# A retention layer and a two-layer MLP on one core: new written-out orders for all engines, and no-operations spread between single matmuls

## The chip, the cores and the metric

The kernel runs on one core of a Trainium2 chip. The core has a matrix engine (TensorE, "PE" in the profile; its weight loads are shown apart as "PEld"), VectorE (DVE), ScalarE (ACT), GpSimd (POOL) and a queue engine that here only issues DMAs (SyncE, "SP"). The metric is the device time of one execution in microseconds, the median of several.

## The reference

Inputs are float32: q, k, v of shape (8, 8, 576, 64), that is 8 batches, 8 heads, 576 positions of 64 numbers; `w_in` of 512 x 2048 and `w_out` of 2048 x 512. What is computed:

```python
scores = (q @ k^T) / 8                               # per batch and head, 576 x 576
D[i, j] = gamma_h ** (i - j) if i >= j else 0        # gamma_h = 1 - 2 ** (-5 - h)
x = heads side by side of (scores * D) @ v           # 4608 tokens x 512
out = square(relu(x @ w_in)) @ w_out                 # 4608 x 512
```

No softmax stands between the two attention products, so the sum over positions can be carried as a state from one chunk of 128 positions to the next. The two products of the MLP are by far the larger part of the arithmetic.

## The kernel before, in words

**Tiling.** The 4608 tokens are cut into 36 units of 128 rows: 32 full chunks (a batch, 128 positions) and 4 units that take the last 64 positions of two batches. Two units make a group; there are 18 groups, 0 to 17. Matmuls run in fp16 with sums in float32. The weights are cast to fp16 on their way in by eight DMAs that POOL issues (L417, `w_in` and `w_out` in four blocks each) and stay on the chip.

**What a group goes through.** POOL (for groups 0 to 3 partly VectorE) scales and casts k, q and v (L455, L470, L476; in groups 0 to 3 tiles `kx`, `qx`, `vx`, L506). SP issues DMA transposes of q and k (tile `kqT`, L487). PE does the retention: scores into `psc`, masked by VectorE into `rT` (L784), states into `psS`, outputs into `psO`. All of that is matmuls of 64 x 64 quarters of the array, recorded by one helper, `quad` (L441), in tasks that hold 33 to 128 of them in groups 0 to 3. From group 4 on the work of two groups (outputs of one, scores and states of the next) is joined to one task, `f0`, of over 190 instructions; there are 13 such tasks, which the text calls long runs. `psO` is copied out as `xT` (ScalarE L845, VectorE L669).

**First product** (`x @ w_in`, transposed). In ten groups it is plain: 16 blocks of four matmuls, 256 columns wide (L1163), each pair of blocks followed by a relu on ScalarE (L1172) and a square on ScalarE or VectorE (L1179, L1181). In the eight groups of `FSET` (4, 6, 8, 10, 12, 14, 15, 16) it follows Strassen's scheme with seven products: tasks of eight matmuls, 128 columns wide (L1014), whose results ScalarE (L1023) copies and VectorE (L1042) adds.

**Second product** (`g @ w_out`). Group 0 is plain (512 columns wide, L1201, sixteen matmuls for a unit); all others follow Strassen's scheme with matmuls of 256 columns, two to a task (L1256), whose left sides VectorE sums (L1229) and whose results ScalarE (L1271, L1332) copies and VectorE (L1281) adds into `o`; SP stores it (L957, L962).

**Order.** The kernel's functions put 1848 tasks on a list: for each an engine, a function that emits its instructions, the tasks that it needs, the buffers that it acquires and frees, and `size`, the count of its PE instructions (a weight load and a matmul each count). `Schedule.emit` calls the functions in the order of a constant, `ORDER`, which names the tasks by number. The engines take their own instructions in that order and wait on semaphores for those of others; the buffers (eight PSUM banks in pool `ff`, rings of `xT`, `gT`, `kqT` and so on) are given out in the same order.

**No-operations.** `place_runs` goes through the PE tasks in order. Ahead of each long run it takes the next number of `PADS` and spreads so many no-operations (`filler`, an instruction of PE's queue, L335) over the small tasks since the run before: those of `size` up to 8, from the fiftieth PE task on. `emit` writes a task's share as one burst behind the task. In the kernel before, 373 no-operations lie ahead of the first, fifth, twelfth and thirteenth run.

Of the kernel before, what the change touches and what calls it, by code (L numbers as in the profile page):

```python
# [71 lines left out]
""".split()  # L72


class Schedule:
# [45 lines left out]
    def place_runs(self, tasks):  # L121

        def spread(n, among):
            total = sum(x["dur"] for x in among)
# [1278 lines left out]
```

## Time and profile before

| | |
|---|---|
| time, median of 3 runs | 292.0 us (290.43 to 293.24) |
| profiled execution, its own time | 292.98 us |
| its span in the profile | 291.3 us |
| mean granted TensorE clock | 0.995 |
| PE | 276.6 us busy (95%), 4730 matmuls |
| VectorE | 200.8 us (69%), 405 instructions |
| ScalarE | 199.7 us (69%), 374 instructions |
| POOL | 101.1 us (35%), 133 instructions |

The profile is of one execution, whose own time lies 1.7 us above its span and 1.0 us above the median of the runs. Busy time of an engine leaves out its queue's instructions: no-operations, semaphores, branches and the issue of DMAs. Matmuls are pipelined and their ends are modelled, so neighbouring matmuls overlap in the records (a 256-wide one is drawn as 273 ns long, while the next can begin after 109 ns), and short idle times of PE are seen between starts and not in the busy share. In the tables of stretches the columns are: the stretch, its length, busy time and count of PE, PEld, DVE, ACT and POOL, the granted clock, the share of the DMA engines, and GB/s.

### The profile page before, as it was taken

What the parts mean: (1) busy time and instruction counts of PE and PEld (TensorE: products, weight loads), DVE (VectorE), ACT (ScalarE), POOL (GpSimd) and SP (SyncE); (2) the same over time, 40 slices, a digit from 0 to 9 for tenths busy, and PEclk for the clock granted to TensorE, in tenths of its full rate; (3) what the DMA queues carried; (4) which work ended last, traced back from release to release, by engine and by line L of the source; (5) the groups of instructions that cost most, each with busy time, mean ns of one, the idle gap of its engine ahead of it and who ended that gap; (6) DMA issues with size and microseconds to landing.
All of it is one profiled execution on the core that took longest, in us unless ns stands there. A gap on an engine that the chain in (4) does not pass through costs nothing.

```text
span 291.3 us, 11387 instructions
## 1 busy us (share of the span) xinstructions
PE 276.6 (95%) x4730; PEld 236.9 (81%) x4730; DVE 200.8 (69%) x405; ACT 199.7 (69%) x374; POOL 101.1 (35%) x133
## 2 busy tenths in 40 slices
PE   7997999999999999999999999999979999999993
PEld 3575767788899889989798988799959888999882
DVE  4782479998876668567847885857666886664652
ACT  6535987487749766977677578758748667887630
POOL 7560037815526533536253433442434400000000
PEclk9999999999999999999999999999999999999998
DMA  7999998989998999999699798899897901011104
GB/s 208 287 207 205 276 300 177 176 194 204 163 195 214 148 201 198 229 172 190 177 182 200 185 197 177 192 191 205 196 213 181 245 16 38 3 73 37 38 36 144
DMA packets 119153, 50.01 MB, mean 172 GB/s; under 512 B 94784, under 2 KB 113728, under 8 KB 119104
## 3 DMA queue, kind: packets, MB, share of 16 engines
q1 hardware_dynamic: 114560, 44.84, 73.0%
q0 software_dynamic: 4224, 4.19, 8.7%
q8 instruction: 38, 0.62, 0.9%
q10 hardware_dynamic: 320, 0.26, 0.4%
q14 instruction: 11, 0.09, 0.1%
HBM read 36.70 MB, written 9.44 MB: 158 GB/s over the span
## 4 chain that ended last, share of the span: by engine, by line
PE 64%; DMA 11%; DVE 11%; SPq 6%; issue 3%; ACT 2%; POOL 1%; DVEq 0%; POOLq 0%
PE po L1256 27%; PE ph L1163 18%; PE ph L1014 13%; DMA w_out<-in_moe_w_out_dram 4%; DMA kqT<-kq 2%; PE psO L441 2%; PE po L1201 2%; DMA stage<-in_v_dram 2%; DVE stage L1229 2%; DVE rT L784 2%; DMA loads<-in_v_dram 1%; SPq L399 1%; DMA out_dram<-o 1%; SPq L377 1%; DVE gT L1229 1%
## 5 line engine op out<-in xcount | busy, mean ns | idle before, releaser
L1163 PE MATMUL ph<-xT,w_in 128*128 128x256 f16 x640 | 84.4, 273 | 2.0 <-issue 1.8
L1163 PEld LDWEIGHTS <-w_in 128*128 128x128 f16 x640 | 61.1, 98 | 11.4 <-issue 2.5
L1172 ACT ACTIVATE gT<-ph 128x512 f16<-128x512 f32 x80 | 46.8, 596 | 25.3 <-PE ph L1163 25.3
L1256 PEld LDWEIGHTS <-gT 128*128 128x128 f16 x544 | 50.7, 98 | 7.6 <-issue 1.5
L1256 PE MATMUL po<-w_out,gT 128*128 128x256 f16 x272 | 45.1, 273 | 0.3 <-DVE rT L784 0.3
L1256 PE MATMUL po<-wT,gT 128*128 128x256 f16 x272 | 42.1, 273 | 0.3 <-DVE o L1281 0.3
L1256 PE MATMUL po<-wT,stage 128*128 128x256 f16 x272 | 41.8, 273 | 0.1
L1256 PEld LDWEIGHTS <-stage 128*128 128x128 f16 x408 | 37.7, 98 | 5.1 <-DVE stage L1229 0.4
L455 POOL CAST kq<-loads 128x512 f16<-128x512 f32 x28 | 19.2, 686 | 62.9 <-DMA loads<-in_k_dram 62.7
L1179 ACT ACTIVATE gT<-gT 128x512 f16<-128x512 f16 x66 | 39.6, 629 | 0.3
L1042 DVE CUSTOM_DVE_ANT_0 gT<-ph,stage 128x512 f16<-128x512 f32 x32 | 22.0, 687 | 19.4 <-PE ph L1014 14.3
L1014 PEld LDWEIGHTS <-pair_c 128*128 128x128 f16 x512 | 33.0, 98 | 2.5 <-issue 1.1
L1056 ACT ACTIVATE gT<-gT 128x1024 f16<-128x1024 f16 x32 | 33.2, 1056 | 1.3 <-DVE gT L1042 1.0
L470 POOL TENSOR_TENSOR kq<-loads,qexp 128x512 f16<-128x512 f32 x24 | 26.5, 1104 | 19.5 <-DMA loads<-in_q_dram 18.1
L476 POOL TENSOR_TENSOR v<-loads,vdec_full 128x512 f16<-128x512 f32 x24 | 28.0, 1174 | 13.9 <-DMA loads<-in_v_dram 12.7
L1229 DVE TENSOR_TENSOR stage<-gT,stage 128x512 f16<-128x512 f16 (+1 forms) x51 | 31.6, 626 | 0.6
L1023 ACT COPY stage<-ph 128x512 f32<-128x512 f32 x32 | 18.7, 587 | 11.7 <-PE ph L1014 9.9
L1014 PEld LDWEIGHTS <-w_in 128*128 128x128 f16 x384 | 24.8, 98 | 2.2 <-issue 1.0
L1281 DVE TENSOR_TENSOR o<-po,u 128x256 f32<-128x256 f32 x33 | 13.8, 421 | 17.9 <-ACT u L1271 10.9
L1271 ACT COPY u<-po 128x256 f32<-128x256 f32 x34 | 12.7, 373 | 15.6 <-PE po L1256 15.6
L1256 PE MATMUL po<-w_out,stage 128*128 128x256 f16 x136 | 22.6, 273 | 0.0
L845 ACT CAST xT<-psO 128x512 f16<-128x512 f32 x28 | 15.7, 589 | 7.8 <-PE psO L441 7.5
(111 smaller groups left out, 416.2 us busy)
## 6 DMA issues: line engine op xcount, KB each, us to landing
out_dram<-o SPq DMA_DIRECT2D x32, 256.0 KB, 3.6
loads<-in_k_dram SPq DMA_DIRECT2D x24, 256.0 KB, 4.4
loads<-in_q_dram SPq DMA_DIRECT2D x96, 64.0 KB, 3.2
loads<-in_v_dram SPq DMA_DIRECT2D x24, 256.0 KB, 4.2
w_in<-in_moe_w_in_dram POOLq DMA_DIRECT2D x4, 512.0 KB, 8.5
w_out<-in_moe_w_out_dram POOLq DMA_DIRECT2D x4, 512.0 KB, 13.7
pair_c<-in_k_dram SPq DMA_DIRECT2D x2, 512.0 KB
pair_c<-in_q_dram SPq DMA_DIRECT2D x4, 256.0 KB, 6.0
```

The source lines that it names most:

```text
L455: op(out=out_.rearrange("p (n b a d) -> p n b a d", n=2, b=2, a=2), in_=in_.rearrange("p (a n b) d -> p n b a d", n=2, a=2))
L470: nc.gpsimd.tensor_tensor(out=out_.rearrange("p (t a d) -> p a t d", t=4, a=2), in0=tile_of["q32", u].rearrange("p (a t) d -> p a t d", a= ...
L476: nc.gpsimd.tensor_tensor(out=t, in0=tile_of["v32", u], in1=vdec[kind].rearrange("p (h o) -> p h o", o=1).to_broadcast([P, H, D]), op=ALU. ...
L1014: nc.tensor.matmul(out_[:, e], lhsT=left[:, m, fi * P:(fi + 1) * P], rhs=right()[:, m], start=fresh and e == 0 and m == 0, stop=m == HK - ...
L1023: nc.scalar.copy(out=part_at[name], in_=bank(j, "a").rearrange("p e t -> p (e t)"))
L1042: nc.vector._custom_dve(TENSOR_ADD_SAT, out=g_at(s, h, j), in0=bank(j, x), in1=part_at[name].rearrange("p (e t) -> p e t", t=P), s0=3.4028 ...
L1056: nc.scalar.activation(out=t, in_=t, func=ACTF.Square)
L1163: nc.tensor.matmul(tile_of["ph", g, fb][:, j, :], lhsT=w_in16[:, m, fi * P:(fi + 1) * P], rhs=tile_of["x", g][:, m, :], start=(m == 0), st ...
L1172: nc.scalar.activation(out=tile_of["g", g][:, nf * fb:nf * (fb + 1), :], in_=tile_of["ph", g, fb], func=ACTF.Relu)
L1179: nc.scalar.activation(out=t, in_=t, func=ACTF.Square)
L1229: (nc.gpsimd if eng == "POOL" else nc.vector).tensor_tensor(out=S_(k)(sl), in0=in0(sl), in1=in1(sl), op=op)
L1256: nc.tensor.matmul(tile_of["pb", g, bank], lhsT=left(i), rhs=right[:, i, :], start=(start and i == 0), stop=(i == HF - 1), skip_group_chec ...
```

## The change

Three things change; the tasks, their functions, their dependencies and the sizes of all buffers stay.

1. `ORDER` is another order of the same 1848 tasks. On PE 707 of 853 tasks stand at another place in their engine's order, by at most 33 places; on VectorE 269 of 358, on ScalarE 258 of 367, on POOL 51 of 100 (at most 5 places) and on SP 103 of 170 (at most 16).
2. `PADS` has other numbers, in all 888 no-operations instead of 373: ahead of the first, second, fifth, tenth, eleventh, twelfth and thirteenth long run 112, 219, 109, 179, 3, 191 and 75. The list goes on with zeros.
3. The no-operations are spread otherwise. A task's share goes by its `size`, no longer by its planned duration; from the two hundredth PE task on, tasks of `size` up to 16 take a share, which brings in the Strassen first products (L1014), where before only those up to 8 did; and the share is no burst behind the task any more: each matmul of the task calls `tick`, which emits a no-operation whenever the running share has reached one.

In the changed kernel lines move down: the helper `quad` is L445, the no-operation L339, Strassen's first products L1018, plain first products L1169, the plain second product L1208, Strassen's second products L1264.

```diff
@@ -14,61 +14,61 @@
 
 
 ORDER = """
-0 34 1 2 3 35 4 5 6 36 7 8 9 70 10 71 11 37 12 76 72 13 73 78 14 38 77 79 75 40 15 16 80 81 17 18 39 74 19 314 82 20 42 21 315 83 22 41 23 24 316 25
-26 84 43 27 88 317 319 90 318 28 29 85 320 30 323 89 87 86 91 321 324 92 322 44 332 93 325 31 45 32 33 326 327 46 483 328 484 47 487 329 485 488 330
...
+0 34 1 2 3 35 4 5 6 36 7 8 9 70 10 71 11 37 12 76 72 13 73 77 14 38 78 79 75 40 15 16 80 81 17 18 39 74 19 20 314 82 42 21 83 319 315 41 22 23 316 24
+84 88 320 25 85 44 317 26 27 90 28 29 318 30 89 43 31 91 87 323 46 92 321 324 93 86 32 33 325 45 327 48 326 332 328 483 484 322 487 329 485 50 47 488
...
 """.split()
 
 
@@ -110,21 +110,25 @@
                 w["left"] -= 1
         self.place_runs([t for t in order if t["eng"] == "PE"])
         for t in order:
+            self.owed, self.step = 0.0, 2.0 * t["pad"] / max(t["size"], 1)
             t["fn"]()
-            for i in range(t["pad"]):
-                self.filler()
-
-
-    PADS = (121, 0, 0, 0, 68, 0, 0, 0, 0, 0, 0, 125, 59)
+
+    def tick(self):
+        self.owed += self.step
+        while self.owed > 0.999:
+            self.owed -= 1.0
+            self.filler()
+
+    PADS = (112, 219, 0, 0, 109, 0, 0, 0, 0, 179, 3, 191, 75, 0, 0, 0, 0, 0, 0, 0, 0, 0, 0, 0, 0, 0, 0, 0, 0, 0)
     FIRST_PAD = 50
 
     def place_runs(self, tasks):
 
         def spread(n, among):
-            total = sum(x["dur"] for x in among)
+            total = sum(x["size"] for x in among)
             until, done = 0.0, 0
             for x in among:
-                until += x["dur"]
+                until += x["size"]
                 upto = int(n * until / total + 1e-6)
                 x["pad"] += upto - done
                 done = upto
@@ -135,7 +139,7 @@
             if t["size"] > 190:
                 spread(next(pads), between or [t])
                 between = []
-            elif t["size"] <= 8 and i >= self.FIRST_PAD:
+            elif t["size"] <= (16 if i >= 200 else 8) and i >= self.FIRST_PAD:
                 between.append(t)
 
 
@@ -1013,6 +1017,7 @@
                     for m in range(HK):
                         nc.tensor.matmul(out_[:, e], lhsT=left[:, m, fi * P:(fi + 1) * P], rhs=right()[:, m],
                                          start=fresh and e == 0 and m == 0, stop=m == HK - 1, skip_group_check=True)
+                        sched.tick()
             w = [wS_done[k][j]] if k in wS_done else []
...
             users.append(p)
@@ -1070,6 +1075,7 @@
                             for m in range(NP):
                                 nc.tensor.matmul(tile_of["hp", g, fi][:, x, :], lhsT=w_in16[:, m, (fi + x) * P:(fi + x + 1) * P],
                                                  rhs=tile_of["x", g][:, m, :], start=(m == 0), stop=(m == NP - 1))
+                                sched.tick()
                         key = base + F1LEN * (JSTEP * (j if not FIRSTP else 0) + (n + x / 2) / 4 * (1 - JSTEP))
                         ts.append(add("PE", key, 0.4366, f, deps=xs + wcast_of(fi) + ts, acq=() if x else ("ff",), size=8))
                     n += 1
@@ -1162,6 +1168,7 @@
                     for m in range(NP):
                         nc.tensor.matmul(tile_of["ph", g, fb][:, j, :], lhsT=w_in16[:, m, fi * P:(fi + 1) * P],
                                          rhs=tile_of["x", g][:, m, :], start=(m == 0), stop=(m == NP - 1))
+                        sched.tick()
                 f1.append(add("PE", place((nf * fb + j) * n), 0.01 + 0.2133 * n, f,
                               deps=[T["x", u] for u in us] + wcast_of(nf * fb + j) + f1[-1:],
                               acq=("ff",) if j == 0 else (), size=8))
@@ -1200,6 +1207,7 @@
                         tile_of["po", u] = ps_ff.tile([P, DM], FP32, name="po", tag="ff")
                     nc.tensor.matmul(tile_of["po", u], lhsT=tile_of["g", g][:, fi, s * P:(s + 1) * P],
                                      rhs=w_out16[:, fi, :], start=(fi == 0), stop=(fi == NF - 1))
+                    sched.tick()
                 f2.append(add("PE", 95.9 + fi / 1000 if late else base2 + NF * s + fi, 0.216, f, deps=[sq[fi // nf]] + wcast[4 + fi // 4] + f2[-1:],
                               acq=("ff",) if fi == 0 else (), size=2))
 
@@ -1255,6 +1263,7 @@
                     for i in (2 * q, 2 * q + 1):
                         nc.tensor.matmul(tile_of["pb", g, bank], lhsT=left(i), rhs=right[:, i, :],
                                          start=(start and i == 0), stop=(i == HF - 1), skip_group_check=not start)
+                        sched.tick()
                 chain[bank] = [add("PE", at_(key + q), 0.2184, f,
                                    deps=chain.get(bank, []) + deps(q // 2) + (reads if q == 0 else []) + wT_done.get(k, []),
                                    acq=("ff",) + more if start and q == 0 else (), size=4, inside=k > 1)]
```

106 rows, old and new, of the table ORDER are left out of this document.

## The prediction

> **What bounds the kernel.** I read the engines' shares and the chain that ended last, then five stretches, then what stands in the chain beside TensorE.
>
> ```profile
> PE 276.6 (95%) x4730; PEld 236.9 (81%) x4730; DVE 200.8 (69%) x405; ACT 199.7 (69%) x374; POOL 101.1 (35%) x133
> PE 64%; DMA 11%; DVE 11%; SPq 6%; issue 3%; ACT 2%; POOL 1%; DVEq 0%; POOLq 0%
> q8 instruction: 38, 0.62, 0.9%
> ```
> ```profile
> 27.00:80.00 53.00, 52.41 (x801) 42.38 (x802) 42.46 (x70) 39.31 (x77) 22.47 (x23) 1.00 1.00 212
> 80.00:130.00 50.00, 49.16 (x984) 44.68 (x982) 33.77 (x62) 36.29 (x69) 20.38 (x24) 1.00 1.07 196
> 130.00:180.00 50.00, 49.23 (x884) 44.46 (x882) 36.10 (x66) 35.34 (x67) 21.74 (x22) 1.00 0.97 184
> 180.00:230.00 50.00, 47.86 (x958) 42.21 (x956) 35.20 (x62) 35.40 (x65) 20.08 (x24) 1.00 0.93 197
> 230.00:286.00 56.00, 55.32 (x785) 49.75 (x778) 36.34 (x74) 38.10 (x69) 2.49 (x2) 1.00 0.16 52
> ```
> The second column of a stretch is PE's busy time: from 27 to 286 us PE stands for 5.0 us of 259, at a granted clock of 1.00. The change keeps all 4730 matmuls. So the time moves by what happens to PE's gaps, and a gap anywhere counts in full. The largest:
>
> ```profile
> 212.52 0.46 PE psO L441 x48
> 212.98 1.85 PE po L1256 x16
> 214.83 0.11 PE ph L1163
> 214.94 1.82 issue
> 216.77 0.97 PE ph L1163 x7
> ```
> "issue" names no partner. The third line of the first fence does: 38 fetches, 16 KB each, for about 9,855 PE instructions are one per 256. If 64 instructions run ahead of the first of the program, both places where PE stood with no semaphore attached (17.6 and 216.8 us ended them) lie on a multiple of 256. Each border seems to ask for the block after the next: the border was passed at 211.9, the fetch ran from 214.2 to 215.3, PE went on at 216.8, 4.9 us after the border. The run of small attention matmuls (L441, some 9 ns for a weight load and its matmul) had begun at place 195 of its block; so 196 of the next 256 instructions were over in 0.9 us, the rest in 1.9 us, and the next block was not there.
>
> **What the change does to such stalls.** The no-operations before a run shift it in its block. In the new program every run of over 190 instructions starts at places 101 to 141, and at least 107 instructions of its last block are left when it ends; in the kernel before, runs ending at places 72 to 162 brought no such gap. Gain 1.8 us. Ends: 0 (another run stalls instead) and 2.0 (measured between starts).
>
> [...]
>
> **No-operations** rise from 373 to 888. Their price:
>
> ```profile
> L335 PEldq NOP  x11: 13/13/13, 220.6 to 221.3; - x11
> ```
> ```profile
> 220.34 0.61 PE L1014 MATMUL ph<-xT,pair_c 128*128 128x128 f16 x8
> 220.79 0.38 PE L1256 MATMUL po<-wT,stage 128*128 128x256 f16 x2
> 221.01 0.61 PE L1014 MATMUL ph<-xs,pair_c 128*128 128x128 f16 x8
> 221.45 1.04 PE L1163 MATMUL ph<-xT,w_in 128*128 128x256 f16 x8
> 222.33 1.04 PE L1256 MATMUL po<-wT,stage 128*128 128x256 f16 x8
> ```
> Eleven no-operations took 0.73 us from first to last: 72 ns each, although each is drawn as 13 ns; other instructions between them cost 3 to 4 ns. From start to start a 256-wide matmul takes 0.88/8 = 109 ns, a 128-wide first product (L1014) 0.45/8 = 56 ns. As long as the sequencer is ahead, no-operations cost nothing. It is at most 43 instructions ahead, and at each wait it stands until the semaphore comes, which eats the lead. The old spread put none into first products; the new one gives them the same number per matmul as the wide ones.
>
> Stretch by stretch, counted in the new order: before the second long run stand 219 no-operations among 96 first-product and 66 wide matmuls. PE needs 96 x 0.0555 + 66 x 0.109 = 12.5 us; the sequencer 219 x 0.0715 + 324 x 0.0035 = 16.8 us. It is the slower one for the whole stretch: **+4.2 us** (3.5 with cheaper other instructions, 5.5 where waits add to it). Before the 10th and 12th runs the two are even (179: 13.9 against 13.6; 191: 14.8 against 14.4), but a first product with 1.2 no-operations takes 0.09 instead of 0.0555: 56 x 0.036 = 2.0 us each if nothing of it is caught up, 0.4 to 0.8 if the wide ones give it back. 109 and 75 no-operations elsewhere cost 0 to 0.9 each. Together +1.5, ends 0 and 5. The old spread's own cost (starts late by 0.05 to 0.11 us at 217, 225 and 234) goes: -0.3.
>
> **Start.** The chain runs through POOL:
>
> ```profile
> 13.51 1.03 POOL vx L506
> 14.54 1.49 POOL w_in L417 x2
> 16.03 10.95 DMA w_out<-in_moe_w_out_dram
> ```
> ```profile
> PE po L1201 <- DMA w_out<-in_moe_w_out_dram: 1.9, 1, 1.9
> ```
> Two w_in issues now stand ahead of that vx, which waits 1.9 us for its load, so the w_out issues come up to 1.5 us sooner, unless the full DMA engines (share 1.2) eat that. And PE has 21 tasks of first matmuls, not 13, before the first w_out matmul: 8 x 0.437 = 3.5 us more cover than the 1.9 us wait. What is late next: the retention work of groups 2 and 3 behind VectorE, 10.0 of 10 us busy from 50 to 60. Its last vx of group 2 ran at 41.5 to 42.2, and PE would now want it at 41.2. So I take -1.0, ends -1.9 and 0.
>
> **Waits in the middle.** Without the fetch gap PE stands 3.2 us after 27; the page draws a matmul to 273 ns where the next could start after 109, so some 20 gaps hide up to 0.16 us each: about 6 us between starts, 5.6 of it after 60 us. I measured in both orders, for each group of matmuls, the PE work between the matmul that its input comes from and itself, less the ScalarE and VectorE instructions between by their rows (relu 0.60, copies 0.37 and 0.59, sums 0.4 to 0.7). Under 0.25 us are left in 61 of 816 places before, in 21 after. I halve the 5.6: -2.8, ends -4.2 and +1. SP's transposes and stores move by up to 16 places among the same DMAs; POOL waits 62.7 us for loads and so decides little; PE waited for a transpose only at 104.6 and 126.5 (1.0 us, within the 5.6).
>
> **Sum**, against the profiled execution's 292.98 (span 291.3 and 1.7 around it): -1.8 + 4.2 + 1.5 - 0.3 - 1.0 - 2.8 = -0.2. Its own 292.98 is 1.0 above the median of the three runs; from that median, 292.0, I forecast **291.8 us**. Within 1%, 289.1 to 294.9, is about what a measurement can't tell from no change.
>
> **Rivals.** (a) *The order wins.* At 213 to 214.8 the old kernel carried 1.4 no-operations per wide matmul with none late; if the even stretches cost nothing, the dense one 3.5, waits fall to their end and the start gives all: -1.8 + 3.5 - 0.3 - 1.9 - 4.2 = -4.7, 287.3 us. For it: the far fewer tight places. Against: 219 x 72 ns can't be hidden in 12.5 us. (b) *The sequencer starves PE, slower than before.* If waits take its lead at each first product, all of them are paid: 96 x 0.05 = 4.8, twice 2.0, 0.9 and 0.7, in all 10.4 instead of 5.7: +4.5, 296.5 us. It decides once the lead at a first product is under some 10 instructions; the lead after waits in the old kernel was 2 to 10. (c) *The orders are alike*: waits stay at 5.6, +2.6, 294.6. (d) The gap's cause is not the fetch, or a run stalls elsewhere: 293.6.
>
> [...]
>
> **Chances.** Forecast with (c) and (d) near it: same 0.41. Faster by over 1%, (a) and its neighbours: 0.31. Slower, mainly (b): 0.28. Range 287.0 to 297.0, from (a) to (b).
>
> **What would show it.** No "issue" entry over 1 us after 30 us in the chain; in the stretch after the run that in the old kernel began at 75.2 us, first products every 105 ns and no-operations 72 to 80 ns apart; that stretch 16 to 17 us from run to run; PE's first w_out matmul without a DMA wait; half the wait time elsewhere. I am wrong if no-operations cost less than 60 ns there, if VectorE makes new waits before 60 us, or if another run ends in a fetch gap.

## The result, and the profile after

The changed kernel takes 304.6 us (median of 4 runs, 302.9 to 306.2), the kernel before 292.6 us in the same comparison (4 runs, 290.4 to 293.5): ratio 1.042, 95% interval 1.032 to 1.052. It is 12 us slower, where 291.8 us in a range of 287 to 297 was forecast. Medians are of all executions; the ratios and intervals on record leave out those over 1.5% above the fastest of their kernel.

The page of the changed kernel, busy shares, instruction fetches, and the chain that ended last:

```profile
PE 291.1 (96%) x4730; PEld 246.1 (81%) x4730; DVE 204.2 (67%) x405; ACT 199.8 (66%) x374; POOL 104.3 (34%) x133
...
q8 instruction: 40, 0.66, 0.9%
...
PE 78%; DVE 10%; DMA 7%; ACT 2%; issue 1%; POOL 1%; SPq 1%; DVEq 0%
```

The same 4730 matmuls keep PE "busy" 14.5 us longer, and "issue" (time in which PE waited for nothing that the profile shows) falls from 3% to 1%: the gap of 1.8 us is gone, and something slower has come. The five stretches between long runs that have no-operations in the changed kernel show where. The table of stretches, first of the kernel before, then of the changed one (stretch, length, busy time and count of PE, and so on):

```profile
76.20:89.60 13.40, 13.20 (x185) 12.06 (x175) 11.06 (x22) 8.22 (x16) 5.63 (x7) 1.00 1.00 192
116.80:126.20 9.40, 9.40 (x123) 8.40 (x109) 5.30 (x10) 8.67 (x16) 4.39 (x5) 1.00 1.19 215
182.00:197.50 15.50, 15.18 (x181) 13.19 (x169) 10.79 (x20) 10.83 (x22) 6.63 (x7) 1.00 0.90 194
212.80:228.60 15.80, 13.97 (x173) 11.92 (x160) 11.05 (x20) 9.81 (x21) 6.48 (x9) 1.00 0.90 190
229.90:238.50 8.60, 8.47 (x105) 6.99 (x105) 7.33 (x12) 5.99 (x12) 2.49 (x2) 1.00 0.45 127
```
```profile
78.50:98.70 20.20, 20.07 (x176) 15.14 (x174) 11.06 (x22) 8.49 (x16) 11.08 (x12) 1.00 0.97 193
125.60:136.50 10.90, 10.90 (x131) 9.65 (x116) 7.36 (x12) 8.76 (x15) 5.27 (x5) 1.00 1.08 188
193.40:210.20 16.80, 16.70 (x174) 14.23 (x165) 10.54 (x20) 11.28 (x23) 7.71 (x9) 1.00 0.87 183
225.40:244.00 18.60, 18.32 (x183) 14.93 (x178) 12.03 (x22) 12.13 (x25) 5.63 (x7) 1.00 0.69 144
245.10:252.60 7.50, 7.50 (x113) 6.94 (x110) 5.73 (x10) 4.17 (x10) 0.00 (x0) 1.00 0.11 39
```

Read the length, not the busy time: the first stretch has 176 records of matmuls instead of 185 and takes 20.2 us instead of 13.4, and PE is drawn as busy for 20.07 of them, because each matmul is drawn as over 0.2 us long and so covers the pause behind it. VectorE, ScalarE and POOL have less than 0.6 of the stretch. No engine is the bound; PE's sequencer is. The no-operations of that stretch, and the matmuls of a part of it in order of time:

```profile
L339 PEldq NOP  x218: 13/13/13, 78.5 to 98.6; - x109
```
```profile
87.84 0.81 PE L1018 MATMUL ph<-xT,pair_c 128*128 128x128 f16 x6
88.59 0.39 PE L1264 MATMUL po<-wT,stage 128*128 128x256 f16 x2
88.82 1.02 PE L1018 MATMUL ph<-xT,pair_c 128*128 128x128 f16 x8
89.79 0.38 PE L1264 MATMUL po<-wT,stage 128*128 128x256 f16 x2
90.04 1.04 PE L1018 MATMUL ph<-xs,pair_c 128*128 128x128 f16 x8
```

218 no-operations from 78.5 to 98.6 us are one every 92.6 ns, and eight first products take 0.97 us (88.82 to 89.79) where eight took 0.45 before. With the records put in the order of the program, the time from one no-operation to the next is 71 ns if nothing lies between them and 90 to 91 ns if matmuls do, no matter whether one, two or four (in the changed kernel over 600 of the 888 have that interval; the others with matmuls between are longer, hardly any shorter). So a no-operation that stands alone costs 90.5 ns of the sequencer. Of the 218 no-operations of this stretch 193 stood 1 or 2 instructions behind the matmul that PE had just begun: the sequencer had no lead, and PE lived from hand to mouth.

"Lost" below is the sum, over neighbouring matmuls, of the time from start to start beyond the 0.109 or 0.0555 us that such a matmul needs; the need is the length less the loss. "Priced" takes 0.0905 us for a no-operation with matmuls ahead of it and 0.071 for one directly behind another (57 of them in the stretch ahead of the 2nd run, then 5, 27, 31 and none).

| ahead of long run | no-operations | priced, us | PE needs | length | lost | lost before |
|---|---|---|---|---|---|---|
| 2nd | 219 | 18.7 | 12.8 | 20.2 | 7.4 | 0.4 |
| 5th | 109 | 9.8 | 9.9 | 10.9 | 1.0 | 0.0 |
| 10th | 179 | 15.7 | 13.8 | 16.8 | 2.9 | 0.8 |
| 12th | 191 | 16.7 | 14.7 | 18.6 | 3.8 | 2.2 (2.0 the fetch gap) |
| 13th | 75 | 6.8 | 7.1 | 7.4 | 0.4 | 0.7 |

Together 15.5 us against 4.1, so +11.4 of the +13.2 us of span. The priced times come 1 to 2 us short of the length in the three large stretches: some intervals between no-operations are longer than either price, in the second stretch 19 of them with a single matmul and no semaphore between. What makes them longer was not found.

Up to the first long run it is +2.2 (75.15 to 77.36 us), behind the last -0.8, and +0.4 lies between. Up to the first long run PE has a new wait, in the changed kernel's waits of PE and of VectorE (who waits, for whom, us, times, longest), and VectorE in order of time:

```profile
PE ph L1169 <- DVE stmp L608: 2.3, 1, 2.3
```
```profile
DVE wT L944 <- DMA w_out<-in_moe_w_out_dram: 6.2, 2, 5.6
```
```profile
29.89 0.69 DVE L944 TENSOR_TENSOR wT<-w_out 128x1024 f16<-128x1024 f16 x1 [5.62 <-DMA w_out<-in_moe_w_out_dram]
30.50 0.42 DVE L608 TENSOR_TENSOR stmp<-psS,R 128x256 f32<-128x256 f32 x1
```

PE's first products need the PSUM bank that `stmp` frees. In the new order `stmp` stands in VectorE's queue behind a `wT` difference that needs the second block of w_out. So PE waits for w_out after all, through VectorE, although it has first products left to do: 2.3 us, where the kernel before waited 1.9 us for w_out itself. In this profile PE then ran at half rate from 32.2 to 35.6 us (0.213 us from start to start; granted clock 0.63 from 31 to 35.5), which is some 1.7 us more and most of the +2.2.

### The profile page after: what moved, and what is told of

It is laid out like the page before. It is cut to its first block, busy times and chain, and to the rows that moved or that the text cites. A ratio compares the mean times of both kernels' runs of the same rounds, so it can differ in the third digit from the quotient of the medians.

```text
span 304.5 us, 11906 instructions
## 1 busy us (share of the span) xinstructions
PE 291.1 (96%) x4730; PEld 246.1 (81%) x4730; DVE 204.2 (67%) x405; ACT 199.8 (66%) x374; POOL 104.3 (34%) x133
## 4 chain that ended last, share of the span: by engine, by line
PE 78%; DVE 10%; DMA 7%; ACT 2%; issue 1%; POOL 1%; SPq 1%; DVEq 0%
PE po L1264 32%; PE ph L1018 19%; PE ph L1169 17%; DMA w_out<-in_moe_w_out_dram 4%; PE psO L445 3%; PE po L1208 2%; DMA pair_c<-in_v_dram 2%; DVE stage L1237 2%; DVE rx L586 2%; PE psc L445 1%; DVE pair_c L982 1%; PE psS L445 1%; ACT gT L1061 1%; PE psT L532 1%; DVE R L559 1%
## 5 line engine op out<-in xcount | busy, mean ns | idle before, releaser
L1169 PE MATMUL ph<-xT,w_in 128*128 128x256 f16 x640 | 84.2, 276 | 2.7 <-DVE stmp L608 2.3
L1169 PEld LDWEIGHTS <-w_in 128*128 128x128 f16 x640 | 62.2, 99 | 12.5 <-issue 3.3
L1179 ACT ACTIVATE gT<-ph 128x512 f16<-128x512 f32 x80 | 46.1, 597 | 24.4 <-PE ph L1169 24.0
L1264 PEld LDWEIGHTS <-gT 128*128 128x128 f16 x544 | 51.0, 97 | 8.0 <-issue 0.8
L1264 PE MATMUL po<-w_out,gT 128*128 128x256 f16 x272 | 45.1, 273 | 0.4 <-DVE Rm L809 0.2
L1264 PEld LDWEIGHTS <-stage 128*128 128x128 f16 x408 | 38.0, 97 | 7.0 <-DVE stage L1237 0.5
L1264 PE MATMUL po<-wT,stage 128*128 128x256 f16 x272 | 42.1, 273 | 0.2 <-DVE stage L1237 0.2
L1264 PE MATMUL po<-wT,gT 128*128 128x256 f16 x272 | 41.6, 273 | 0.0
L1018 PEld LDWEIGHTS <-pair_c 128*128 128x128 f16 x512 | 37.0, 97 | 3.6 <-issue 0.4
L480 POOL TENSOR_TENSOR v<-loads,vdec_full 128x512 f16<-128x512 f32 x24 | 29.0, 1212 | 24.1 <-DMA loads<-in_v_dram 19.5
L1047 DVE CUSTOM_DVE_ANT_0 gT<-ph,stage 128x512 f16<-128x512 f32 x32 | 22.0, 686 | 20.3 <-PE ph L1018 20.2
L459 POOL CAST kq<-loads 128x512 f16<-128x512 f32 x28 | 20.8, 742 | 36.0 <-DMA loads<-in_k_dram 31.3
L1018 PEld LDWEIGHTS <-w_in 128*128 128x128 f16 x384 | 27.0, 97 | 4.5 <-issue 1.9
L1028 ACT COPY stage<-ph 128x512 f32<-128x512 f32 x32 | 18.7, 586 | 14.4 <-PE ph L1018 13.5
L1018 PE MATMUL ph<-xs,pair_c 128*128 128x128 f16 x256 | 22.7, 218 | 0.1
L1018 PE MATMUL ph<-xT,w_in 128*128 128x128 f16 x256 | 21.5, 219 | 1.1 <-DVE Rm L809 1.0
## 6 DMA issues: line engine op xcount, KB each, us to landing
w_out<-in_moe_w_out_dram POOLq DMA_DIRECT2D x4, 512.0 KB, 14.5
```

The lines of the kernel that those rows point to most:

```text
L459: op(out=out_.rearrange("p (n b a d) -> p n b a d", n=2, b=2, a=2), in_=in_.rearrange("p (a n b) d -> p n b a d", n=2, a=2))
L480: nc.gpsimd.tensor_tensor(out=t, in0=tile_of["v32", u], in1=vdec[kind].rearrange("p (h o) -> p h o", o=1).to_broadcast([P, H, D]), op=ALU. ...
L1018: nc.tensor.matmul(out_[:, e], lhsT=left[:, m, fi * P:(fi + 1) * P], rhs=right()[:, m], start=fresh and e == 0 and m == 0, stop=m == HK - ...
L1028: nc.scalar.copy(out=part_at[name], in_=bank(j, "a").rearrange("p e t -> p (e t)"))
L1047: nc.vector._custom_dve(TENSOR_ADD_SAT, out=g_at(s, h, j), in0=bank(j, x), in1=part_at[name].rearrange("p (e t) -> p e t", t=P), s0=3.4028 ...
L1169: nc.tensor.matmul(tile_of["ph", g, fb][:, j, :], lhsT=w_in16[:, m, fi * P:(fi + 1) * P], rhs=tile_of["x", g][:, m, :], start=(m == 0), st ...
```

## Experiments

Two questions: is it the no-operations or the order that costs 12 us, and where did the expected gains of the order and of the avoided gap go? The kernel before was timed beside each group of runs, on other chips; its medians were 292.6, 295.7, 292.9, 292.0 and 293.3 us. All ratios are to the runs of the kernel before in the same group. In the second of these groups (`no219`, `no_noops`, `bursts`, `wT_behind`) the kernel before lay between 291.9 and 299.8 us, and the recorded ratios of `no_noops` and `wT_behind`, 0.983 and 1.015, amount to some 298 us for it; by its median of 295.7 they would be 0.990 and 1.024.

### The dense stretch alone

```diff
-    PADS = (112, 219, 0, 0, 109, 0, 0, 0, 0, 179, 3, 191, 75, 0, ...
+    PADS = (112, 0, 0, 0, 109, 0, 0, 0, 0, 179, 3, 191, 75, 0, ...
```

> The changed kernel with the 219 no-operations ahead of the second long run left out (second number of PADS 0), nothing else. All later runs then start 37 places later in their blocks of 256 (139 to 178 instead of 102 to 141); the most instructions of a run in one block are 179, where the stalled run of the kernel before had 196. Theory 1 (each no-operation that stands alone costs PE's sequencer 90 ns, so 219 of them set the pace of the dense stretch): the 7.35 us that PE lost between matmuls in the stretch from 78.5 to 98.7 us go to under 0.6, and the time falls by 6.6 us, from 304.6 to about 298.0. Theory 2 (the new order's own waits make the loss; the no-operations fill time that PE would wait anyway): the stretch stays within 1.5 us of its 20.2 us and the time above 302.

298.5 us, ratio 1.013 (1.008 to 1.018). The stretch in this kernel's table:

```profile
78.20:91.00 12.80, 12.80 (x179) 11.91 (x168) 9.71 (x20) 8.32 (x16) 4.84 (x6) 1.00 0.87 168
```

12.8 us, with nothing lost: 7.4 us of the loss were those 219 no-operations, as theory 1 said, and the time is within 0.5 us of what it expected.

### All no-operations out of the changed kernel

```diff
+    PADS = (0, 0, 0, 0, 0, 0, 0, 0, 0, 0, 0, 0, 0, 0, ...
```

> The changed kernel with all numbers of PADS 0: no no-operation is left but the 13 fixed ones. The 14.6 us that PE lost in the five padded stretches go. By the fetch theory (a block of 256 instructions comes about 4.9 us after the border before the last, so a block that holds more than some 176 quick instructions of a run ends in a gap) ten of the 13 long runs then lie badly (193 to 254 of their instructions in one block) and bring gaps of 0.9 to 3.7 us each, together some 20 us: 304.6 - 14.6 + 20 = 310, between 304 and 315, with about ten gaps of over 0.8 us without a semaphore behind runs. If the gap of the kernel before was not the fetch, no such gaps come: 290. If the order sets the time: within 2 of 304.6.

292.8 us, ratio 0.983 (0.976 to 0.990), and in a second group 294.8 us, 1.009 (1.005 to 1.013):

> The changed order without no-operations once more, now beside the old order without them on one chip. Theory (without no-operations the new order is the better one: its waits are shorter): 291.5 to 294.5, 4 to 7 us below the old order without no-operations. Rival (the 6 us between the two came from two chips): within 2 us of it.

So the no-operations cost about 10 to 12 us net, nearly all that the change lost, and the expectation of 310 was wrong. The gaps that the fetch theory asked for are there, but smaller. In the order of the program, every gap after 27 us of over 0.35 us that has neither a semaphore nor more than two no-operations in it begins behind instruction 192 or 193 of a block of 256, counted from PE's first, in all 17 traces: the border as the prediction counts it. Counted by that place (gaps of over 0.2 us; a wait that falls there is counted too), the second run had six, 0.6 to 1.6 us long, 6.0 in all; the first four, 2.8 in all. Its waits of PE, and PE around the longest:

```profile
PE po L1264 <- issue: 1.9, 2, 1.4
PE psO L445 <- issue: 1.3, 2, 0.7
```
```profile
172.57 0.61 PE L1018 MATMUL ph<-xT,w_in 128*128 128x128 f16 x8
173.02 0.27 PE L1264 MATMUL po<-wT,stage 128*128 128x256 f16 x1
174.69 0.50 PE L1264 MATMUL po<-wT,stage 128*128 128x256 f16 x3 [1.39 <-issue]
```

The instruction fetch ran from 172.30 to 173.41 us, and PE went on 1.28 us after its end. Of the 52 gaps at that place in all traces 51 ended 1.1 to 1.6 us after a fetch did.

### Bursts instead of single no-operations

```diff
-            self.owed, self.step = 0.0, 2.0 * t["pad"] / max(t["size"], 1)
+            self.owed, self.step = 0.0, 0.0
             t["fn"]()
+            for i in range(t["pad"]):
+                self.filler()
```

> The changed kernel with its order, its PADS and its shares by size, but a task's share written as one burst behind the task, as in the kernel before. Every instruction of a run keeps its place in its block. Theory 1a (in the traces a no-operation behind another takes 71 ns, one with matmuls between takes 90.5 however many they are, so a burst of n costs n x 71 + 19.5): the dense stretch needs 219 x 0.071 + 42 bursts x 0.0195 = 16.4 us instead of 20.2, the ones ahead of the tenth, twelfth and fifth runs lose 2.4, 3 and 0.9 less: 304.6 - 10 = 295, between 293 and 298. Theory 1b (the 90 ns are the price of any no-operation while matmuls run): no change, 303 to 306.

299.1 us, ratio 1.013 (1.007 to 1.019): 5.8 below the changed kernel (304.9, next but one), in the direction of theory 1a, but less than its 10 and outside the 293 to 298 that it gave. The no-operations of 4.5 us of the dense stretch:

```profile
L341 PEldq NOP  x58: 13/13/13, 88.0 to 92.5; - x58
```

58 in 4.5 us are one in 79 ns instead of 92.6. The five stretches lost 4.9, 0.2, 0.9, 2.0 and 0.0 us, 7.9 instead of 15.5. That is 7.6 less, of which 5.8 came through; this trace also has half rate behind PE's early wait (granted clock 0.76 from 31 to 36 us) and a wait of 1.8 us at 53.3, which the changed kernel's traces do not have. What a burst costs beyond n x 71 + 19.5 (17.8 us in the dense stretch, 16.4 expected) was not found.

### VectorE's wT behind stmp

```diff
 ORDER = """
-... 512 494 63 567 561 335 516 568 ...
+... 512 494 567 561 335 63 516 568 ...
```

> The changed kernel with one task of VectorE moved: the first difference of w_out blocks (wT, it waits for the second w_out block) goes behind the sum of states (stmp) that frees a PSUM bank for PE's first products. Theory: PE's 2.4 us wait at 28.4 us is VectorE's queue, blocked by that wT, and the half clock from 31 to 35.7 us (0.213 us from start to start of a 256-wide matmul) follows from the wait. Both go: -2.4 in each execution, -2 more in those that showed the lower clock; 304.6 to about 301, between 299.5 and 302.5, with no matmul after 20 us at half rate. Rival: the first w_out matmul then waits for its block (it landed at 27 in the kernel before), or the VectorE wait turns up at the next bank; the time stays within 1 of 304.6.

302.9 us (302.2 to 303.2), ratio 1.015 (1.008 to 1.022), 2.0 below the changed kernel and 0.4 above the range expected. The wait is gone, and the first long run starts at 73.9 us, 3.5 earlier than in the changed kernel's first profile, 1.5 earlier than in its second (below), which had no half rate, and 1.3 earlier than in the kernel before.

### The changed kernel once more

No edit.

> The changed kernel as it is, beside the runs that leave a part of it out, because the kernel before took 295.7 us there and 292.6 in the first comparison. If that difference belongs to the chip and adds to all, 307 us; if the early part of the kernel before alone varies (its first w_out block and PE's wait for it), 303 to 306. From its median the leaving-out runs are read: left out 219 no-operations, it should stand 6 to 8 us above the 298.5 of that run; with bursts instead of single ones, 5 to 8 above 299.1; with wT behind stmp, 2 to 4 above 302.9.

304.9 us (304.4 to 305.4), ratio 1.040 (1.033 to 1.047). The dense stretch lost 7.1 us again, the five 15.3. This time no half rate followed PE's early wait, and the first long run started at 75.35 us.

### The old order without no-operations, and with the dense stretch

```diff
-    PADS = (121, 0, 0, 0, 68, 0, 0, 0, 0, 0, 0, 125, 59)
+    PADS = (0, 0, 0, 0, 0, 0, 0, 0, 0, 0, 0, 0, 0)
```

> The kernel before with all numbers of PADS 0, so that both orders can be compared without no-operations (the changed order took 292.8). Theory 1: the gap of 2.0 us at 214.7 was made by the 125 no-operations behind that run, which carry the sequencer to the next border sooner, and gaps without no-operations are about 0.85 us each and need some 220 instructions of a run in one block (the changed order without no-operations showed 0.88, 0.82 and 0.82 us, at 229, 225 and 254 of them, none at 214 and fewer). Here four runs have 231, 222, 225 and 250: 1.7 to 3.4 us of gaps, and none at the others (212 and fewer). So the time stays within 1.5 of the kernel before on the same chip, and the new order is worth 1 to 4 us. Theory 2 (the orders are alike): 292 to 293.5.

> The old order without no-operations, beside the new one without them. Theory: 297 to 300, with waits of PE on VectorE and ScalarE of over 5 us behind 27 us, where the new order has some 7 less 2.5 of its early wait. Rival: 292 to 294.

298.8 us, ratio 1.022 (1.012 to 1.031), and 297.5, 1.018 (1.012 to 1.024). The first missed what was expected: not within 1.5 us of the kernel before, but 6.0 above it. In the second group the changed order without no-operations stood beside it at 294.8, 2.7 us lower. That is less than the 4 to 7 expected. The gaps on the block border were 3.2 and 7.4 us in the two traces, against 2.0 with the old no-operations, so gaps are much of the 5 to 6 us, and the old no-operations had been worth having.

Next, the order of the kernel before with the new spreading and 219 no-operations ahead of the second run:

```diff
-    PADS = (121, 0, 0, 0, 68, 0, 0, 0, 0, 0, 0, 125, 59)
+    PADS = (121, 219, 0, 0, 68, 0, 0, 0, 0, 0, 0, 125, 59, 0, ...
```

> The order of the kernel before with the new way of spreading (single no-operations, first products included, by size) and its PADS but for 219 ahead of the second long run. Theory 1 (the no-operations cost the same in any order): the stretch between the first and the second run grows from 13.4 to 219 x 0.0905 = 19.8 us, +6.5; the gap of 2.0 us at the eleventh run goes, since it now starts at place 158 with 159 of its instructions in one block: about +4.5 against the kernel before. Theory 2 (it is the new order that makes them costly, by waits that take the sequencer's lead): +1 or less.

301.8 us, ratio 1.029 (1.022 to 1.036), in its table of stretches:

```profile
77.60:97.90 20.30, 20.26 (x183) 15.30 (x172) 13.28 (x22) 8.42 (x16) 8.67 (x10) 1.00 0.85 195
```

20.3 us and 7.3 lost, in the old order as in the new: theory 1. The whole grew by 8.9, not 4.5; another gap of 1.1 us on a block border came at the thirteenth run, which this PADS moved, and PE waited 1.9 us for VectorE's `rT` at 195 us.

### The order freed of both faults

First with 44 no-operations, then with none:

```diff
 ORDER: 63 behind 335
+    PADS = (0, 0, 0, 0, 0, 0, 0, 0, 0, 44, 0, 0, 0, 0, ...      # wT_44
+    PADS = (0, 0, 0, 0, 0, 0, 0, 0, 0, 0, 0, 0, 0, 0, ...       # wT_0, wT_0_2
```

> The changed order without its no-operations, with the wT task of VectorE behind stmp, and with 44 single no-operations ahead of the tenth long run alone, which move the tenth to thirteenth runs from 225, 254, 194 and 180 instructions in one block to 212, 215, 150 and 193. Theory: the wait of 2.5 us at 27.9 us goes, the gaps of 0.82 us at 201.9 and 215.6 go, and the 44 no-operations cost under 0.2 us among 152 matmuls; 292.8 - 2.5 - 1.6 = 288.7, between 287.5 and 290.5. Rival: the early wait comes back at the next semaphore and the gaps stay: 291.5 to 293.

293.1 us, ratio 0.999 (0.994 to 1.003): a miss. The tenth run, which the 44 were to free, showed a gap of 2.3 us at the border inside it: its fetch began only at 199.92 us, when PE already stood.

> The changed order without no-operations, with wT behind stmp. In the run with 44 no-operations that move brought the first long run forward from 75.3 to 73.7 us, and a gap of 2.3 us behind a late instruction fetch at 199.9 took it back. Theory: without that gap (here 0.8 as without the move) 1 to 2 us faster than without the move: 290.5 to 292. Rival: what is gained early is waited for later, since VectorE and ScalarE set the pace behind: within 0.7 us of the run without the move.

> The changed order without no-operations and with wT behind stmp, again: 290.5 to 292.5 if two loads of a kernel agree within 1 us; with gaps on fetch borders of 3 to 6 us in its trace.

291.4 us, ratio 0.996 (0.992 to 1.0005), and 291.4, 0.999 (0.995 to 1.003): both as expected, and no measurable difference to the kernel before. Their gaps on the block border were 4.8 and 6.4 us.

### The kernel before, built again

No edit.

> The kernel before, for a second trace of it: its runs spread from 291.6 to 298.1 us, those of the changed kernel from 302.9 to 306.2 in four, those without no-operations by 2. Theory (a block of instructions comes between some 2.9 and 4.9 us after its border, by chance; the eleventh run at place 195 and the tenth at 194 leave no margin): the gap behind the eleventh run differs by over 0.5 us from the 2.0 of the first trace, or another long run shows one. Rival (the spread comes from the first w_out block): the gap is 1.8 to 2.2 again, and PE's start after 27 us differs.

> The kernel before as it is. If the 1.8% between two builds of it belongs to that one load, 291 to 294, with semaphore waits of PE behind 27 us of some 5 us in its trace; if this kernel simply spreads between loads, 294 to 299 with 8 us or more of such waits.

298.2 us, ratio to the first build 1.018 (1.010 to 1.025), and 294.7, 0.997 (0.992 to 1.002); the twelve executions of the third build lie between 289.1 and 298.7 us. The largest waits of PE after 27 us in the second build's trace, then in the third's:

```profile
PE ph L1014 <- DVE rT L784: 2.9, 3, 2.2
```
```profile
PE ph L1014 <- DVE rT L784: 2.1, 3, 1.4
PE ph L1014 <- DVE Rm L805: 1.7, 2, 1.5
```

Counted between starts, the third build's semaphore waits after 27 us are 10.0 us and the second's 10.6, against 4.8 in the trace that the prediction was made from. But these two profiled executions took 296.7 and 300.1 us, longer than the medians of their own runs; they show how a long execution of this kernel spends its time, and say nothing of the median. The gap at the eleventh run was 1.3 us in the second build and 0.5 in the third instead of 2.0. Why one build came out 1.8% slower than another of the same code was not found.

The longest of these waits has a place, though. VectorE ahead of it in the second build, and at the same point in the first trace:

```profile
189.11 1.88 DVE L1229 TENSOR_TENSOR stage<-gT,stage 128x512 f16<-128x512 f16 x2
190.91 1.52 DVE L1229 TENSOR_TENSOR gT<-gT 128x1024 f16<-128x1024 f16 x1
```
```profile
184.60 0.75 DVE L1229 TENSOR_TENSOR stage<-gT,stage 128x512 f16<-128x512 f16 x2
185.27 0.68 DVE L1229 TENSOR_TENSOR gT<-gT 128x1024 f16<-128x1024 f16 x1
```

The same instructions took 2.0 us longer. POOL worked beside them from 188.5 to 191.9 us in the second build; in the first trace it was idle from 184.4 to 186.5. This holds throughout: after 60 us the 17 traces have 381 VectorE instructions over 0.3 us longer than the median of their form, every one of them with a POOL instruction beside it, and none among the 2999 that had no POOL instruction beside them. The first trace of the kernel before has 15 of them, those of the second and third build 23 and 25. The number alone does not set the time (the fastest kernel below has 25 too), and no experiment moved POOL's work, so it is not shown that this makes one execution longer than another.

### No-operations only where there is time for them

```diff
 ORDER: 63 behind 335
+    PADS = (100, 0, 0, 0, 80, 0, 0, 0, 0, 0, 0, 100, 0, 0, ...
```

> The changed order, wT behind stmp, and 280 single no-operations in place of 888: 100 ahead of the first long run, 80 ahead of the fifth, 100 ahead of the twelfth. No long run then has over 193 of its instructions in one block (10 of 13 under 170). Theory: where the stretch has time for n x 0.09 us (7.2 of 10.3 us, 9 of 14.7) single no-operations cost under 0.5 us each stretch, and the gaps without a semaphore on the fetch border (0.98, 0.96, 0.93, 0.51 and 1.06 us in the run without no-operations) fall to under 1.5 us in all: 288 to 290, 2 to 4 us below wT_0_2 beside it. Rival (PE's time goes to VectorE and ScalarE, and a gap that goes comes back as a wait): within 1 of it.

287.0 us (286.4 to 287.6), ratio 0.9805 (0.977 to 0.984), 4.4 below the same order without no-operations and below the 288 to 290 expected: faster than both kernels, with six runs within 1.2 us. It is one build; the kernel before, built again, once came out 1.8% off itself, so the places below carry the claim, not the time alone. Its page and all of PE's waits of over 0.25 us after 27 us:

```profile
PE 276.0 (97%) x4730; PEld 238.2 (83%) x4730; DVE 203.9 (71%) x405; ACT 199.0 (70%) x374; POOL 102.8 (36%) x133
```
```profile
PE po L1264 <- DVE stage L1237: 0.5, 1, 0.5
PE po L1264 <- DVE Rm L809: 0.4, 2, 0.2
PE ph L1169 <- DVE stmp L813: 0.4, 1, 0.4
PE ph L1018 <- DVE Rm L809: 0.4, 1, 0.4
PE psS L445 <- POOL vx L510: 0.3, 1, 0.3
PE po L1264 <- DVE o L1290: 0.3, 1, 0.3
```

No "issue" is left: not one gap of over 0.2 us lies on a block border. The stretches with 80 and 100 no-operations lost 0.4 and 0.6 us, semaphore waits included. Against the first trace of before the span is 5.4 us shorter: 1.6 up to the first long run, 3.0 from there to the last (2.0 of them the gap), 0.8 behind it.

## Why the prediction was wrong

**The step that failed is the price of the no-operations.** The prediction had 72 ns each and 3 to 4 ns for other instructions, from a row of eleven: 16.8 us for the dense stretch, +4.2, and +1.5 for the others. A no-operation with matmuls ahead of it costs 90.5 ns: the dense stretch took 20.2 us and lost 7.4, and the tenth, twelfth and fifth stretches, which I had called even or free, lost 7.7 us together. In the dense stretch first products came every 121 ns (0.97 us for eight) and no-operations every 92.6, not every 105 and 72 to 80. The row held the right price: in the order of the program its eleven are a burst of six and one of five with four matmuls between, and the one interval with matmuls in it is 91 ns long, eight of the nine others 70 or 71. I took the mean as the price, and most of the new no-operations stand alone.

By the two prices the three large stretches lose (18.7 - 12.8) + (15.7 - 13.8) + (16.7 - 14.7) = 9.8 us, not 5.7; measured are 14.1. The other 4.3 are the longer intervals whose cause stays open. Of the 13.4 us between the forecast change of -0.2 and the +13.2 of the span, 7.8 lie in the five stretches, 3.2 ahead of the first long run and 2.4 in the rest. The experiments show the first part: without the 219 the dense stretch takes 12.8 us, without any the kernel is 10 to 12 us faster, and 219 in the old order cost that stretch the same 7 us.

**Rival (b) named the mechanism** (the sequencer starves PE) and its sign, at 296.5; it had all losses at 10.4 where 15.5 came, for the same wrong price. Its condition, a lead under some 10 instructions at the first products, is what the trace shows (1 or 2 instructions at 193 of the 218 no-operations).

**The fetch gap went, as forecast.** The eleventh run has none, and the changed kernel's two traces have 0.7 and 1.1 us at block borders. But its price was not a property of the run's place alone (by that the changed order without no-operations should have had 20 us of gaps, and had 3 to 6). The experiments without no-operations bear out the cause: four to seven gaps a trace, always at one place of the block, PE going on 1.1 to 1.6 us after a fetch. Why a fetch comes as late as it does (once, in `wT_44`, only when PE already stood) stays open. In all, the gaps at block borders came to up to 7.4 us in a trace (`before_no_noops_2`).

**Start: -1.0 forecast, +0.2 and +2.2 measured;** the 2.0 between the two are mostly the half rate, which came in one of the two traces. A new wait on VectorE before 60 us was one of the prediction's own signs of being wrong. PE had the extra first products, but I had not followed the bank that they wait for: VectorE's `wT` ahead of `stmp`. I had looked for what is late next between 41 and 60 us; it was at 28.4. Nor did w_out come sooner for its earlier issue (15.5 instead of 16.0 us): the weights' queue had half of its packets landed by 22.8 us in the kernel before and by 23.2 in the changed one. With `wT` behind `stmp` the step holds: in five traces the first long run starts 0.6 to 1.7 us earlier than in the kernel before.

**Waits in the middle: -2.8 forecast, -0.4 measured** in the span outside the five stretches and the start. Counted as waits it is 4.8 us in the trace that I used and 3.5 in the changed kernel without the early wait. I had halved 5.6 us on a count of tight places; how much a tight place is worth stays open.

**As a sum, what I had put down for the order and the avoided gap**, 5.6 us (1.8 + 1.0 + 2.8), lies near the 6.3 us by which the kernel with few no-operations is faster than the kernel before beside it. That needed one task moved on VectorE, and no-operations only in stretches with time for them, and 4.4 of the 6.3 came with the no-operations, which took away 6.4 us of gaps where the forecast had 1.8. So the nearness of the two sums is luck, not a proof of the terms.

## What to carry to other kernels

Price an instruction that does nothing as it will stand: take it from a place in the trace where the same neighbours stand on both sides, count it against the time of the engine behind the queue in that stretch, and put none where that sum comes near. Padding that moves a dense run away from a fetch border paid here only in stretches with time to spare (80 and 100 no-operations lost 0.4 and 0.6 us there, 219 in the dense stretch 7.4); 280 such no-operations did the work here that 888 did at a loss of 15 us. When tasks change places in an engine's queue, follow what each long wait there holds up behind it, and read more than one execution before pricing waits of under a microsecond.

## What the hardware showed that was not expected

- A no-operation in PE's queue takes 71 ns of the sequencer behind another and 90.5 ns with matmuls between, one as much as four; it is drawn as 13 ns. PE is drawn as busy while it starves (20.07 of 20.20 us), since drawn matmuls (219 and 273 ns long) cover pauses up to their own length.
- Instruction fetches were not hidden behind a dense run here: gaps of 0.2 to 2.3 us at one place in each 256 instructions, 51 of 52 ending 1.1 to 1.6 us after a fetch. Without no-operations they summed to 2.8 and 6.0 us in two executions of the new order, 3.2 and 7.4 in two of the old.
- After PE had waited 2.3 to 2.9 us at some 28 us, two of six traces with that wait (the changed kernel's first and the one with bursts) show half rate for 3.4 us, four do not. The second build of the kernel before shows it too, behind its wait of 2.0 us for w_out. What decides whether half rate follows such a wait was not shown.
- VectorE instructions took up to 0.9 us longer than others of their form, in 381 cases, only ever with a POOL instruction beside them (17 traces, after 60 us).
- The same code, built and loaded again, came out at 1.018 of itself. Differences of 1 to 2% between single builds were not taken as shown here, unless a trace showed their place.
